# Low parts by a negated copy and an adding transfer instead of a VectorE subtraction, in an attention + bilinear-FFN kernel on one core

## The chip, the core and the metric

The kernel runs on one core of one Trainium2 chip. The metric is the device time of one execution in microseconds (us). Before the change it is 1257.21 us, the median of three runs (1253.98 to 1257.85).

## The reference

```python
# attention: q, k, v are (8, 8, 576, 64); causal by blocks of 64
scores = np.matmul(q, k.transpose(0, 1, 3, 2)) / np.sqrt(D)
scores = np.where(block_i >= block_j, scores, -1e9)
attn = exp(scores - max) / (sum + 1e-09)
x = np.matmul(attn, v)  ->  (4608, 512)
# bilinear feed-forward, d_ff = 1536
a = x @ w_a
b = x @ w_b
out = (a * b) @ w_out            # (4608, 512)
```

Everything is fp32, and the three weights come as doubles of 64 bits that the kernel converts itself.

## The kernel before, in words

**Low parts.** TensorE takes its operands in a rounded form (fp32r). To keep fp32 accuracy, every operand is held twice: a high part, which is the value rounded by ScalarE (a cast), and a low part, which is the value less its high part, by a subtraction on VectorE. A product is then three matmuls: high by high, high by low, low by high. The low parts are made at `split` (L113, of h and of w_out), at L177 and L178 (of the weights and of sums of weights) and at L689 to L692 (of x and sums of x).

**Stages.** For some 640 us attention for 64 heads runs together with the first pass of the feed-forward: tiles of 288 tokens, f 0 to 3 of 12 (f counts blocks of 128 of d_ff). In that pass `ab_unit` makes `h = a*b` (L241 copies a, L243 multiplies to hf, L110 and L113 make hh and hl of it), and `o_unit` multiplies hh and hl by w_out (L217, tile pso). The end of that pass has no attention beside it and runs to about 693 us. Then comes the second stage: two passes of six token tiles of 768 tokens (two halves of 384), pass 0 with f 4 to 7, pass 1 with f 8 to 11. For each f `pair_unit` (L711, tiles psy, psx, psw, psv) makes a and b for both halves with seven products in place of eight, which needs sums of rows of x (seven rows in place of four) and sums of pieces of the weights. VectorE and ScalarE combine the four results to h (L728 to L739). Then `pair_out` (L757, tile pso_z) runs 96 matmuls. In pass 0 the result is added to the DRAM tensor part by transfers that GpSimd issues (L820); in pass 1 SyncE loads part back (L814), VectorE adds it (L822) and SyncE stores the output (L823).

**Sums of x.** `sums_x` works on one of two pairs of the four blocks of 128 rows of x (kp 0 and 1; a block is xr, 128x768). SyncE loads xr (L666) into one of four buffers. VectorE makes four sums of 128x384 (L676, L677, L680, L683; one of them in place), ScalarE casts the seven rows to xh (L681, L682, L684, L685: 768, 768, 768 and 384 columns), and VectorE makes xl by four subtractions of the same sizes (L689 to L692). The next load into a buffer waits for the last reader of what is there.

**Conversion of weights.** A weight tile of 128x512 doubles comes by SyncE (L124, raww). `convert` turns it into fp32 by six instructions, five on VectorE between L139 and L149 and one on ScalarE (L140), through work tiles s, m and x (sw, mw, xw in the profile), with one buffer each. For f 4 and up `sums` reuses m for four sums of 128x128 (L172, four small instructions), ScalarE casts the plain pieces (L165) and the sums (L175) to the high parts, and VectorE subtracts for the low parts (L177 of 128x384, L178 of 128x512). The weights of f 4 to 7, eight such tiles and four of w_out, are converted from the end of attention on: `background` hands out 48 steps as the first pass goes on, one per STEP ns of TensorE time, and what is left beside the first tile of the second stage. Those of f 8 to 11 are converted beside pass 0 in the same way at a slower pace (STEP2), put down in DRAM, and loaded again for pass 1 (`staged`).

**What sets the order.** Each engine runs its own instructions in the order that a scheduler fixes when the kernel is built; it goes by the order in which the code is written and by costs of its own. Nothing overtakes on an engine, so an instruction that waits holds all behind it. An instruction can be held behind others by hand (`behind_of`: conversions and low parts go after the last hf).

Of the kernel before, what the change touches and what calls it, by code (L numbers as in the profile page):

```python
# [11 lines left out]
I32 = mybir.dt.int32  # L12
U16 = mybir.dt.uint16
AF = mybir.ActivationFunctionType
ALU = mybir.AluOpType
AX = mybir.AxisListType

P = 128
# [19 lines left out]
XFB = 2  # L38
MORE = 6
PREF = True  # L40
STEP = 800
STEP2 = 3200
LATE = 1
LO2 = lambda nc: nc.vector
# [8 lines left out]
def attention_then_bilinear_ffn(  # L53
# [10 lines left out]
    nc = tc.nc  # L64
# [34 lines left out]
    wpool = pool(ctx, "wpool", 1)  # L99
# [5 lines left out]
    def f32(ap):  # L105
        return ap.bitcast(F32)

    def split(hi, lo, src, hi_eng, lo_eng):
# [3 lines left out]
            hi_eng.tensor_copy(hi, src)  # L112
        return lo_eng.tensor_tensor(lo, src, f32(hi), op=ALU.subtract)  # L113

    last = {}

    def behind_of(ins, key):
# [9 lines left out]
    def convert(raw, nm, paced):  # L127

        hi, mid = raw[:, :, 1], raw.bitcast(U16)[:, :, 1]
        s, m, x = (wpool.tile([P, 512], I32, tag=f"cv_{x}", name=f"{x}{nm}") for x in "smx")  # L130
        sf, mf, xf = (t.bitcast(F32) for t in (s, m, x))
        v = nc.vector

        def step(ins):
            if paced:
                behind_of(ins, "hf")


        step(v.tensor_scalar(s, hi, 20, 0x7FF, op0=ALU.logical_shift_right, op1=ALU.bitwise_and))  # L139
        nc.scalar.activation(s, s, AF.Relu, scale=2.0 ** 23, bias=shift)  # L140
        yield

        step(v.tensor_scalar(m, hi, 0xFFFFF, 0x100000, op0=ALU.bitwise_and, op1=ALU.bitwise_or))
        yield
        step(v.scalar_tensor_tensor(mf, mid, 2.0 ** -16, m, op0=ALU.mult, op1=ALU.add))
        yield
        step(v.scalar_tensor_tensor(s, hi, -0x80000000, s, op0=ALU.bitwise_and, op1=ALU.bitwise_or))  # L147
        yield
        step(v.tensor_tensor(xf, mf, sf, op=ALU.mult))  # L149
        return xf, mf  # L150
# [7 lines left out]
    def new_wo(f):  # L158
        w_sb[f][1] = wopool.tile([P, 2, DO], F32R, tag="wo", name=f"wo{f}")

    def sums(hi, lo, xf, t, paced):

        x, t = (y.rearrange("p (q n) -> p q n", n=P) for y in (xf, t))
        v = nc.vector
        nc.scalar.copy(hi[:, :3], x[:, 1:])  # L165
        for d, a, b, op in (
            (0, x[:, 0], x[:, 3], ALU.add),
            (1, t[:, 0], x[:, 1], ALU.subtract),
            (2, x[:, 1], x[:, 0], ALU.subtract),
            (3, x[:, 2], t[:, 1], ALU.subtract),  # L170
        ):
            ins = v.tensor_tensor(t[:, d], a, b, op=op)  # L172
        if paced:
            behind_of(ins, "hf")
        nc.scalar.copy(hi[:, 3:], t)  # L175
        yield
        v.tensor_tensor(lo[:, :3], x[:, 1:], f32(hi[:, :3]), op=ALU.subtract)  # L177
        v.tensor_tensor(lo[:, 3:], t, f32(hi[:, 3:]), op=ALU.subtract)  # L178

    def convert_w(todo, lo_eng, paced=False, stage=None):  # L180

        def ahead(f, i):
            return fetch(wab[f, :, i] if i < KP else wo[f], f"w{f}_{i}")

        raw = ahead(*todo[0])
        for k, (f, i) in enumerate(todo):
            now, raw = raw, ahead(*todo[k + 1]) if k + 1 < len(todo) else None
            xf, spare = yield from convert(now, f"w{f}_{i}", paced)
            if stage:
                st = stage.tile([P, 2, NW if i < KP else NO, P], F32R, tag="st", name=f"st{f}_{i}")  # L190
            if i == KP:
                if not stage and w_sb[f][1] is None:
                    new_wo(f)
                o = st.rearrange("p j c n -> p j (c n)") if stage else w_sb[f][1]
                split(o[:, 0], o[:, 1], xf, nc.scalar, lo_eng)
            elif f < F1:
                ab = w_sb[f][0]
                hi, lo = (ab[:, j, i].rearrange("p c n -> p (c n)") for j in range(2))
                split(hi, lo, xf, nc.scalar, lo_eng)
            else:  # L200
                ab = st if stage else w_sb[f][0][:, i]
                yield from sums(ab[:, 0], ab[:, 1], xf, spare, paced)
            if stage:
                f -= F1 + F2
                nc.sync.dma_start(wod[f] if i == KP else wabd[f, i], f32(st).rearrange("p j c n -> p (j c n)"))
            yield
# [463 lines left out]
    def sums_x(raw, kp, nm):  # L670

        hi = xk.tile([P, NW, T2], F32R, tag="xh", name=f"xh_{nm}_{kp}", bufs=3)
        t = tpool.tile([P, 3, T2], F32, tag="xt", name=f"xt_{nm}_{kp}")
        a, b = raw[2 * kp:2 * kp + 2]
        v = nc.vector
# [9 lines left out]
        nc.scalar.copy(hi[:, 6], t[:, 2])  # L685
        yield
        lo = xk.tile([P, NW, T2], F32R, tag="xl", name=f"xl_{nm}_{kp}", bufs=2)
        for ins in (
                v.tensor_tensor(lo[:, 0:2], a, f32(hi[:, 0:2]), op=ALU.subtract),  # L689
                v.tensor_tensor(lo[:, 2:4], t[:, :2], f32(hi[:, 2:4]), op=ALU.subtract),  # L690
                v.tensor_tensor(lo[:, 4:6], b, f32(hi[:, 4:6]), op=ALU.subtract),
                v.tensor_tensor(lo[:, 6], t[:, 2], f32(hi[:, 6]), op=ALU.subtract)):  # L692
            if nm[0] == "0" and nm != "0_0":
                behind_of(ins, "hf")
        yield hi, lo
# [95 lines left out]
    stage = pool(left, "stage", 1, reuse_waits="tile")  # L791
# [113 lines left out]
```

## Time and profile before

| what | value |
|---|---|
| median of the runs | 1257.21 us |
| the profiled execution | 1258.86 us |
| its span | 1257.0 us |
| mean granted clock of TensorE | 0.996 |
| busy PE / PEld / DVE / ACT / POOL | 1231.1 / 1172.9 / 977.1 / 704.2 / 427.7 us |
| from 100 to 600 us (500 us): PE, DVE, ACT, POOL busy | 492.38, 400.83, 401.59, 309.46 us |

PE is TensorE's matmuls and PEld its weight loads; DVE is VectorE, ACT ScalarE, POOL GpSimd, SP SyncE. A row of a timeline has the start, the duration, the engine, the line, the operation and its tiles (out<-in), and in brackets the idle time before it and what ended that. Starts of neighbours in a row lie closer together than their durations, since instructions overlap a little: the distance of two starts is called the pitch. Times count from the start of the span.

### The profile page before, as it was taken

Reading aid. Unit: us, or ns where it says so; the run is one execution under the profiler, and the core shown is the slowest. Engines: PE = TensorE matmul, PEld = TensorE weight load, DVE = VectorE, ACT = ScalarE, POOL = GpSimd, SP = SyncE. Lnnn points to the kernel's source line nnn. Section 1 sums busy time; section 2 is a strip of 40 time slices with the busy share of each in tenths; the row PEclk is TensorE's granted clock in tenths of the full one; section 3 lists DMA queues with packets and bytes.
Section 4 is the critical chain, followed back from the end, with each engine's and each line's share of the span. In section 5 each row is a group of like instructions: output and inputs, shape, how many; then the busy total and the mean of one; then the engine's idle time right before and its main releaser. Section 6 shows DMA issues by size and latency. Waiting matters only on the chain.

```text
span 1257.0 us, 23355 instructions
## 1 busy us (share of the span) xinstructions
PE 1231.1 (98%) x7849; PEld 1172.9 (93%) x7849; DVE 977.1 (78%) x2471; ACT 704.2 (56%) x1770; POOL 427.7 (34%) x597
## 2 busy tenths in 40 slices
PE   9998999999999999999999999999999999999998
PEld 5667999999999999999999999999999999999998
DVE  6888887877878778777789998787868677677654
ACT  4787887787887878878746444244235223222210
POOL 3666665665665656656510021021021000000000
PEclk9899999999999999999999999999999999999999
DMA  5467667776677666776233354464378453143131
GB/s 181 119 182 201 173 174 190 183 178 173 162 186 177 176 172 165 186 177 171 68 121 125 128 147 122 117 164 127 112 210 265 151 151 105 50 148 113 39 101 63
DMA packets 86584, 187.14 MB, mean 149 GB/s; under 512 B 11200, under 2 KB 46016, under 8 KB 86464
## 3 DMA queue, kind: packets, MB, share of 16 engines
q1 hardware_dynamic: 74944, 166.76, 47.5%
q0 software_dynamic: 6912, 9.44, 4.6%
q10 hardware_dynamic: 4608, 9.44, 2.1%
q8 instruction: 63, 1.03, 0.4%
q14 instruction: 57, 0.47, 0.1%
HBM read 87.03 MB, written 47.19 MB: 107 GB/s over the span
## 4 chain that ended last, share of the span: by engine, by line
PE 78%; DVE 11%; DMA 4%; ACT 3%; issue 2%; POOL 2%; SPq 0%; ACTq 0%; DVEq 0%; POOLq 0%
PE pso_z L757 14%; PE ps L217 11%; PE psx_z L711 8%; PE psw_z L711 8%; PE psv_z L711 7%; PE tp L468 7%; PE pso L217 5%; PE s L392 4%; PE psy_z L711 4%; PE av L517 3%; PE av L523 3%; PE sl L392 2%; DMA kp<-kT 2%; DVE nm L398 1%; DVE sw L147 1%
## 5 line engine op out<-in xcount | busy, mean ns | idle before, releaser
L217 PE MATMUL ps<-xh,wab 128*128 128x288 f32 x1024 | 241.7, 304 | 1.2 <-ACT a L241 1.2
L757 PE MATMUL pso_z<-h_z,wo 128*128 128x384 f32 x1152 | 202.3, 335 | 0.0
L757 PEld LDWEIGHTS pso_z<-h_z,wo 128*128 128x128 f32 x1152 | 199.9, 188 | 0.1
L445 POOL TENSOR_SCALAR e<-e,rc 128x512 f32<-128x512 f32 (+3 forms) x256 | 151.1, 602 | 130.2 <-DVE rc L442 122.3
L217 PEld LDWEIGHTS ps<-xh,wab 128*128 128x128 f32 x1024 | 172.1, 189 | 4.7 <-ACT a L241 1.4
L472 DVE TENSOR_TENSOR al<-tp,ah 128x512 fp32r<-128x512 f32 x224 | 131.4, 608 | 30.5 <-ACT ah L470 30.0
L217 PE MATMUL ps<-xl,wab 128*128 128x288 f32 x512 | 154.1, 301 | 0.0
L110 ACT CAST h_z<-u_z 128x384 fp32r<-128x384 f32 x96 | 49.3, 513 | 172.4 <-DVE u_z L736 160.7
L470 ACT CAST ah<-tp 128x512 fp32r<-128x512 f32 x224 | 116.4, 531 | 50.9 <-PE tp L468 47.8
L468 PE MATMUL tp<-ident,e 128*128 128x128 f32 x832 | 134.7, 276 | 9.0 <-POOL e L445 3.0
L820 POOL DMA_DIRECT2D part<-pt x48 | 42.0, 943 | 292.6 <-ACT pt L819 292.2
L217 PE MATMUL pso<-hh,wo 128*128 128x288 f32 x512 | 127.2, 310 | 1.0 <-ACT hh L110 0.8
L468 PEld LDWEIGHTS tp<-ident,e 128*128 128x128 f32 x832 | 99.9, 141 | 23.3 <-issue 10.0
L401 ACT ACTIVATE e<-s,nm 128x192 f32<-128x192 f32 (+2 forms) x192 | 101.4, 528 | 35.9 <-DVE nm L398 26.7
L711 PE MATMUL psx_z<-xh,wab 128*128 128x384 f32 x384 | 116.4, 339 | 2.6 <-DVE u_z L729 2.5
L711 PE MATMUL psv_z<-xh,wab 128*128 128x384 f32 x384 | 116.4, 338 | 1.4 <-DVE u_z L738 0.7
L711 PE MATMUL psw_z<-xh,wab 128*128 128x384 f32 x384 | 116.1, 338 | 0.0
L398 DVE TENSOR_REDUCE nm<-s 128x1 f32<-128x192 f32 (+3 forms) x256 | 109.8, 431 | 2.4
L217 PEld LDWEIGHTS ps<-xl,wab 128*128 128x128 f32 x512 | 96.5, 189 | 3.4
L217 PEld LDWEIGHTS pso<-hh,wo 128*128 128x128 f32 x512 | 88.0, 191 | 2.7 <-ACT hh L110 1.4
L392 PE MATMUL s<-k,q 128*128 128x256 f32 x336 | 81.1, 322 | 2.2 <-ACT e_s L401 2.0
L113 POOL TENSOR_TENSOR v<-vr,v 128x320 fp32r<-128x320 f32 x56 | 50.2, 897 | 88.1 <-ACT v L110 69.4
(143 smaller groups left out, 2872.8 us busy)
## 6 DMA issues: line engine op xcount, KB each, us to landing
k<-kp SPq DMA_DIRECT2D x112, 288.0 KB, 3.6
xr<-xd SPq DMA_DIRECT2D x48, 384.0 KB, 4.0
q<-qp SPq DMA_DIRECT2D x112, 160.0 KB, 2.7
raww<-wab SPq DMA_DIRECT2D x24, 512.0 KB, 3.7
qp<-qT SPq DMA_DIRECT2D x32, 320.0 KB, 3.2
vr<-vm SPq DMA_DIRECT2D x64, 160.0 KB, 3.1
kp<-kT SPq DMA_DIRECT2D x32, 288.0 KB, 3.5
xd<-xf ACTq DMA_DIRECT2D x32, 288.0 KB, 3.1
```

The lines of the kernel that those rows point to most:

```text
L110: nc.scalar.copy(hi, src)
L113: return lo_eng.tensor_tensor(lo, src, f32(hi), op=ALU.subtract)
L217: mm = nc.tensor.matmul(ps, w_, d_, start=(i == 0), stop=(i == n - 1))
L392: mark = nc.tensor.matmul(ps[:, :w], qm[:, q0[t]:q0[t] + P], kk[:, :w], start=(i == 0), stop=(i == len(ks) - 1))
L398: nc.vector.tensor_reduce(nm[:, t:t + 1], view, axis=AX.X, op=ALU.max, negate=True)
L401: nc.scalar.activation(out, view, AF.Exp, bias=bias, accum_out=sm[:, t, :1])
L445: nc.gpsimd.tensor_scalar(ev, ev, rc[:, t:t + 1], 1.0, op0=ALU.mult, op1=ALU.mult)
L468: mark = nc.tensor.transpose(tp[:, c], src, ident)
L470: nc.scalar.copy(ah[:, :m, cols], tp[:, :m])
L472: return nc.vector.tensor_tensor(al[:, :m, cols], tp[:, :m], f32(ah[:, :m, cols]), op=ALU.subtract)
L711: nc.tensor.matmul(ps, wt[:, i, iw], j[:, ix], start=start and kp == 0 and i == 0 and j is xh, stop=kp == KP - 1 and i == 1, skip_group_ch ...
L757: nc.tensor.matmul(ps, wt[:, a, osl], b, start=i == 0, stop=i == 3 * len(fs) - 1)
```

## The change

Where the low part is made by the new helper `low`, ScalarE writes the rounded negative of the value, and a transfer from GpSimd's queue then adds the value itself to that, in place: -round(v) + v is the same low part. This is used at two places: for the second pair of rows of x (kp 1) in all 12 tiles (four subtractions on VectorE each become four ScalarE instructions and four transfers of 384, 384, 384 and 192 KB), and for the sums in the eight weight tiles of f 4 to 7 (L178, 128x512, becomes one ScalarE instruction and one transfer of 256 KB). The low parts of the first pair, of the plain pieces of weights, of w_out, of h and of the staged weights stay subtractions. The work tile m, which the transfers read, gets two buffers in place of one. STEP goes from 800 to 700, so the 48 conversion steps are handed out closer together. The memory for the descriptors of GpSimd's transfers is halved, from 16384 (the default) to 8192 bytes. Lines below the helper move by 5 to 8.

```diff
@@ -38,7 +38,7 @@
 XFB = 2
 MORE = 6
 PREF = True
-STEP = 800
+STEP = 700
 STEP2 = 3200
 LATE = 1
 LO2 = lambda nc: nc.vector
@@ -112,6 +112,11 @@
             hi_eng.tensor_copy(hi, src)
         return lo_eng.tensor_tensor(lo, src, f32(hi), op=ALU.subtract)
 
+    def low(lo, whole):
+
+        nc.scalar.mul(lo, whole, -1.0)
+        nc.gpsimd.dma_start(f32(lo), whole, accum_op=ALU.add)
+
     last = {}
 
     def behind_of(ins, key):
@@ -127,7 +132,7 @@
     def convert(raw, nm, paced):
 
         hi, mid = raw[:, :, 1], raw.bitcast(U16)[:, :, 1]
-        s, m, x = (wpool.tile([P, 512], I32, tag=f"cv_{x}", name=f"{x}{nm}") for x in "smx")
+        s, m, x = (wpool.tile([P, 512], I32, tag=f"cv_{x}", name=f"{x}{nm}", bufs=1 + (x in "m")) for x in "smx")
         sf, mf, xf = (t.bitcast(F32) for t in (s, m, x))
         v = nc.vector
 
@@ -158,7 +163,7 @@
     def new_wo(f):
         w_sb[f][1] = wopool.tile([P, 2, DO], F32R, tag="wo", name=f"wo{f}")
 
-    def sums(hi, lo, xf, t, paced):
+    def sums(hi, lo, xf, t, paced, staged):
 
         x, t = (y.rearrange("p (q n) -> p q n", n=P) for y in (xf, t))
         v = nc.vector
@@ -175,7 +180,10 @@
         nc.scalar.copy(hi[:, 3:], t)
         yield
         v.tensor_tensor(lo[:, :3], x[:, 1:], f32(hi[:, :3]), op=ALU.subtract)
-        v.tensor_tensor(lo[:, 3:], t, f32(hi[:, 3:]), op=ALU.subtract)
+        if staged:
+            v.tensor_tensor(lo[:, 3:], t, f32(hi[:, 3:]), op=ALU.subtract)
+        else:
+            low(lo[:, 3:], t)
 
     def convert_w(todo, lo_eng, paced=False, stage=None):
 
@@ -199,7 +207,7 @@
                 split(hi, lo, xf, nc.scalar, lo_eng)
             else:
                 ab = st if stage else w_sb[f][0][:, i]
-                yield from sums(ab[:, 0], ab[:, 1], xf, spare, paced)
+                yield from sums(ab[:, 0], ab[:, 1], xf, spare, paced, stage)
             if stage:
                 f -= F1 + F2
                 nc.sync.dma_start(wod[f] if i == KP else wabd[f, i], f32(st).rearrange("p j c n -> p (j c n)"))
@@ -685,11 +693,11 @@
         nc.scalar.copy(hi[:, 6], t[:, 2])
         yield
         lo = xk.tile([P, NW, T2], F32R, tag="xl", name=f"xl_{nm}_{kp}", bufs=2)
-        for ins in (
-                v.tensor_tensor(lo[:, 0:2], a, f32(hi[:, 0:2]), op=ALU.subtract),
-                v.tensor_tensor(lo[:, 2:4], t[:, :2], f32(hi[:, 2:4]), op=ALU.subtract),
-                v.tensor_tensor(lo[:, 4:6], b, f32(hi[:, 4:6]), op=ALU.subtract),
-                v.tensor_tensor(lo[:, 6], t[:, 2], f32(hi[:, 6]), op=ALU.subtract)):
+        for at, whole in ((slice(0, 2), a), (slice(2, 4), t[:, :2]), (slice(4, 6), b), (6, t[:, 2])):
+            if kp:
+                low(lo[:, at], whole)
+                continue
+            ins = v.tensor_tensor(lo[:, at], whole, f32(hi[:, at]), op=ALU.subtract)
             if nm[0] == "0" and nm != "0_0":
                 behind_of(ins, "hf")
         yield hi, lo
@@ -892,7 +900,7 @@
                     .reshape(NF, P, NCC // 2, -1)).view(np.int64),
         "wo": flat(moe_w_out.reshape(NF, P, -1)).view(np.int64),
     }
-    nc = bacc.Bacc("TRN2", target_bir_lowering=False, num_devices=1)
+    nc = bacc.Bacc("TRN2", target_bir_lowering=False, num_devices=1, dynamic_dma_scratch_size=8192)
     args = [
         nc.dram_tensor(n, a.shape, mybir.dt.from_np(a.dtype), kind="ExternalInput").ap()
         for n, a in arrays.items()
```

VectorE's row has 56 instructions fewer, ScalarE's and GpSimd's 56 more each, SyncE's as many as before.

On VectorE in the second conversion (tile 1 of f 4, at about 651 to 656 us in the trace; `mw_1`, `sw_1`, `xw_1` are its work tiles, `mw_0` and `sw_0` those of the conversions next to it), before:

```order
L147 SCALAR_TENSOR_TENSOR sw_1_9941<-raww_1_9860,sw_1_9941 128x512
L680 TENSOR_TENSOR xt_0_0_10466<-xr_0_9851,xr_0_9849 128x384
L149 TENSOR_TENSOR xw_1_9943<-mw_1_9942,sw_1_9941 128x512
L683 TENSOR_TENSOR xt_0_0_10466<-xr_0_9851,xt_0_0_10466 128x384
L172 TENSOR_TENSOR mw_1_9942<-xw_1_9943 128x128 x2
L172 TENSOR_TENSOR mw_1_9942<-mw_1_9942,xw_1_9943 128x128
L177 TENSOR_TENSOR wab_9845<-xw_1_9943,wab_9845 128x384
L172 TENSOR_TENSOR mw_1_9942<-xw_1_9943,mw_1_9942 128x128
L139 TENSOR_SCALAR sw_0_10015<-raww_0_9939 128x512
L676 TENSOR_TENSOR xt_0_1_10481<-xr_0_9855,xr_0_9853 128x384
L178 TENSOR_TENSOR wab_9845<-mw_1_9942,wab_9845 128x512
```

and now, with what each instruction waits for (`DMASW0` is the landing of the first transfer into wab, issued for `mw_0_9863`):

```order
L152 SCALAR_TENSOR_TENSOR sw_1_9934<-raww_1_9860,sw_1_9934 128x512
L113 TENSOR_TENSOR hl_0_0_9962<-hf_0_0_9959,hh_0_0_9961 128x288 [waits Activation_49]
L154 TENSOR_TENSOR xw_1_9936<-mw_1_9935,sw_1_9934 128x512 [waits DVE_49]
L148 TENSOR_SCALAR mw_0_10004<-raww_0_9932 128x512 [waits DMAHW6_49,DMASW0_49]
L177 TENSOR_TENSOR mw_1_9935<-xw_1_9936 128x128 [waits DVE_49]
L177 TENSOR_TENSOR mw_1_9935<-xw_1_9936 128x128
L177 TENSOR_TENSOR mw_1_9935<-mw_1_9935,xw_1_9936 128x128 [waits DVE_49]
L182 TENSOR_TENSOR wab_9845<-xw_1_9936,wab_9845 128x384 [waits Activation_49]
L177 TENSOR_TENSOR mw_1_9935<-xw_1_9936,mw_1_9935 128x128 [waits DVE_49]
L144 TENSOR_SCALAR sw_0_10003<-raww_0_9932 128x512
```

The subtraction L178 is gone, and the first write of the third conversion's m stands ahead of the second conversion's sums; it waits for the transfer that reads the first conversion's m.

On VectorE at the end of the first pass (hl_1_3 is the last low part of h there; `xl_0_0` and `xl_0_1` are the low parts of the first tile of x), before:

```order
L243 TENSOR_TENSOR hf_1_3_10448<-ps_7_1_3_10426,a_1_3_10424 128x288
L143 TENSOR_SCALAR mw_1_10388<-raww_1_10309 128x512
L147 SCALAR_TENSOR_TENSOR sw_1_10387<-raww_1_10309,sw_1_10387 128x512
L145 SCALAR_TENSOR_TENSOR mw_1_10388<-raww_1_10309,mw_1_10388 128x512
L113 TENSOR_TENSOR hl_1_3_10451<-hf_1_3_10448,hh_1_3_10450 128x288
L149 TENSOR_TENSOR xw_1_10389<-mw_1_10388,sw_1_10387 128x512
L689 TENSOR_TENSOR xl_0_0_10475<-xr_0_9849,xh_0_0_10465 128x768
L172 TENSOR_TENSOR mw_1_10388<-xw_1_10389 128x128 x2
L172 TENSOR_TENSOR mw_1_10388<-mw_1_10388,xw_1_10389 128x128
L177 TENSOR_TENSOR wab_9848<-xw_1_10389,wab_9848 128x384
L172 TENSOR_TENSOR mw_1_10388<-xw_1_10389,mw_1_10388 128x128
```

and now:

```order
L177 TENSOR_TENSOR mw_1_10347<-xw_1_10348,mw_1_10347 128x128
L113 TENSOR_TENSOR hl_1_2_10425<-hf_1_2_10422,hh_1_2_10424 128x288
L251 TENSOR_TENSOR hf_1_3_10456<-ps_7_1_3_10443,a_1_3_10441 128x288
L144 TENSOR_SCALAR sw_2_10578<-raww_2_10344 128x512
L148 TENSOR_SCALAR mw_2_10579<-raww_2_10344 128x512
L150 SCALAR_TENSOR_TENSOR mw_2_10579<-raww_2_10344,mw_2_10579 128x512
L113 TENSOR_TENSOR hl_1_3_10459<-hf_1_3_10456,hh_1_3_10458 128x288
L700 TENSOR_TENSOR xl_0_0_10483<-xr_0_9849,xh_0_0_10473 128x768
L700 TENSOR_TENSOR xl_0_0_10483<-xt_0_0_10474,xh_0_0_10473 128x768
L700 TENSOR_TENSOR xl_0_0_10483<-xr_0_9851,xh_0_0_10473 128x768
L700 TENSOR_TENSOR xl_0_0_10483<-xt_0_0_10474,xh_0_0_10473 128x384
```

The last of the eight conversions (into wab_9848) now stands ahead of the last hf and hl, behind which it stood before, and the first of w_out has begun. The four subtractions for xl_0_1, which followed those for xl_0_0, are gone.

On SyncE in a tile of pass 1 (`xr_3` are the four blocks of x for the tile after the next: 14350, 14352 the first pair and 14354, 14356 the second), before:

```order
L666 DMA xr_3_14350<-xd 128x768
L666 DMA xr_3_14352<-xd 128x768
L666 DMA xr_3_14354<-xd 128x768
L666 DMA xr_3_14356<-xd 128x768
L823 DMA outT<-pt_0_1_1_13989 128x384
L823 DMA outT<-pt_1_1_1_13991 128x384
L823 DMA outT<-pt_2_1_1_13993 128x384
L823 DMA outT<-pt_3_1_1_13995 128x384
```

and now:

```order
L674 DMA xr_3_14394<-xd 128x768
L674 DMA xr_3_14396<-xd 128x768
L831 DMA outT<-pt_0_1_1_14029 128x384
L831 DMA outT<-pt_1_1_1_14031 128x384
L674 DMA xr_3_14398<-xd 128x768
L822 DMA pt_2_1_1_14230<-part 128x384
L822 DMA pt_3_1_1_14237<-part 128x384
L831 DMA outT<-pt_2_1_1_14033 128x384
L831 DMA outT<-pt_3_1_1_14035 128x384
L674 DMA xr_3_14400<-xd 128x768
```

The two loads of the second pair, whose buffers are now read by the adding transfers, stand behind stores of the output and loads of part.

## Prediction

> **What bounds the kernel now.** The page's first part comes first, then the busy time by stretches, PE's waits in the second stage, and the timelines of PE and DVE where those waits lie.
>
> ```profile
> PE 1231.1 (98%) x7849; PEld 1172.9 (93%) x7849; DVE 977.1 (78%) x2471; ACT 704.2 (56%) x1770; POOL 427.7 (34%) x597
> ...
> 640.00:660.00 20.00, 19.49 (x145) 19.04 (x144) 19.53 (x44) 8.51 (x21) 2.17 (x2) 1.00 0.33 105
> 660.00:680.00 20.00, 20.00 (x151) 19.79 (x150) 19.51 (x49) 10.83 (x25) 0.00 (x0) 1.00 0.39 128
> 680.00:700.00 20.00, 18.40 (x113) 17.93 (x112) 19.32 (x41) 12.60 (x25) 0.00 (x0) 0.91 0.49 162
> 700.00:720.00 20.00, 18.48 (x104) 17.39 (x103) 19.79 (x41) 6.80 (x12) 0.00 (x0) 1.00 0.32 106
> ...
> 1000.00:1050.00 50.00, 50.00 (x287) 50.00 (x286) 34.77 (x64) 11.72 (x21) 0.00 (x0) 1.00 0.33 95
> ```
>
> The columns of a stretch are its length, then busy time of PE, PEld, DVE, ACT, POOL, then PE's clock. PE is the bound nearly everywhere. Only from 680 to 720 us does it idle, 1.6 + 1.5 us, and there its clock is at 0.91 for one slice, which costs 20 x 0.09 = 1.8 us more. From 640 to 720 us DVE is full (19.3 to 19.8 of 20): that is where the weights of f 4 to 7 are converted beside the end of the first pass. Late in the second stage DVE has 15 us of 50 free, and work taken from it there is worth nothing by itself.
>
> ```profile
> PE psx_z L711 <- DVE u_z L729: 2.5, 2, 1.6
> PE pso L217 <- DVE hl L113: 1.1, 2, 0.8
> PE pso L217 <- ACT hh L110: 0.8, 1, 0.8
> PE psv_z L711 <- DVE u_z L738: 0.7, 1, 0.7
> PE psv_z L711 <- ACT u_z L728: 0.7, 1, 0.7
> ...
> 684.67 0.40 PE L217 MATMUL pso<-hl,wo 128*128 128x288 f32 x1 [0.77 <-DVE hl L113]
> ...
> 686.29 0.66 PE L217 MATMUL pso<-hh,wo 128*128 128x288 f32 x3 [0.83 <-ACT hh L110]
> ```
>
> The waits after 640 us come to 5.8 us (total, times, longest). With the slow slice that is some 7.6 us, and no relief of DVE can give more than this. The two waits of the timeline, at 684 to 686, are for h's parts, which stand behind conversions on DVE.
>
> **The change, part by part.** The durations are those of the profiled execution, which took 1258.86 us (span 1257.0); it lies 1.65 above the median of 1257.21.
>
> *Weights (8 conversions, f 4 to 7).* First the pitch of the steps on DVE:
>
> ```profile
> 646.71 0.28 DVE L172 TENSOR_TENSOR mw<-xw,mw 128x128 f32<-128x128 f32 x1
> ...
> 660.27 0.55 DVE L177 TENSOR_TENSOR wab<-xw,wab 128x384 fp32r<-128x384 f32 x1
> 660.74 0.28 DVE L172 TENSOR_TENSOR mw<-xw,mw 128x128 f32<-128x128 f32 x1
> 660.94 0.42 DVE L139 TENSOR_SCALAR sw<-raww 128x512 int32<-128x512 int32 x1
> 661.28 0.45 DVE L113 TENSOR_TENSOR hl<-hf,hh 128x288 fp32r<-128x288 f32 x1
> 661.65 0.55 DVE L683 TENSOR_TENSOR xt<-xr,xt 128x384 f32<-128x384 f32 x1
> 662.12 0.68 DVE L178 TENSOR_TENSOR wab<-mw,wab 128x512 fp32r<-128x512 f32 x1
> 662.72 0.68 DVE L147 SCALAR_TENSOR_TENSOR sw<-raww,sw 128x512 int32<-128x512 int32 x1
> ...
> 687.11 0.45 DVE L113 TENSOR_TENSOR hl<-hf,hh 128x288 fp32r<-128x288 f32 x1
> 688.08 0.95 DVE L689 TENSOR_TENSOR xl<-xr,xh 128x768 fp32r<-128x768 f32 x1
> ...
> L175 ACT CAST wab<-mw 128x512 fp32r<-128x512 f32 x8 | 5.0, 620 | 4.4 <-DVE mw L172 4.4
> ```
>
> From start to start L178 occupies 0.60 us, so 8 x 0.60 = 4.8 us leave DVE. In its place ACT does a second pass over 128x512, 0.62 like the cast of L175 (pipelined 0.52), and POOL sends 256 KB. But the transfer still reads m. The next writer of that buffer, two conversions on, waits for it to land, and everything behind that writer on DVE waits too, h's parts of the first pass among it. I walked the changed order of DVE with the pitches above (0.34 for the 128x512 tensor-scalar, 0.60 for 128x512, 0.47 for 128x384, 0.37 for 128x288, 0.20 for 128x128). From the last sum of one conversion to the write of the same buffer lie 4.9, 4.0, 5.3, 5.7, 4.8, 4.1, 5.9, 5.5 us of work. The loop to be covered is 0.1 + 0.52 + 0.52 on ACT plus issue to landing.
>
> No accumulate into the on-chip memory is in the trace. The nearest rows are those into part:
>
> ```profile
> part<-pt POOLq DMA_DIRECT2D x1, 192.0 KB, 4.4
> ...
> part<-pt POOLq DMA_DIRECT2D x1, 192.0 KB, 5.0
> ...
> part<-pt POOLq DMA_DIRECT2D x1, 192.0 KB, 5.2
> ...
> part<-pt POOLq DMA_DIRECT2D x1, 192.0 KB, 7.8
> ...
> 731.64 3.71 POOL L820 DMA_DIRECT2D part<-pt  x4 [87.32 <-ACT pt L819]
> 735.84 0.86 POOL L820 DMA_DIRECT2D part<-pt  x1 [0.49 <-ACT pt L819]
> ```
>
> The DMA issues, looked at one by one, give from issue to landing 4.4 for the one at 731.64, 5.0 and 5.2 for those that come after an idle queue at 776.54 and 916.93, and 7.8 for the fifth of the burst, at 735.84. So a lone one takes 4.4 to 5.2. A burst drains at (735.84 + 7.8 - 731.64 - 4.4) / 4 = 1.9 us each. I take 5.0: more bytes, but a nearer target than DRAM. The loop is then 6.1 us, and the stalls are 1.2, 2.1, 0.8, 0, 1.3, 0.7, 0, 0.6 (a stall that both ends share counts once). 6.1 of these 6.7 us come ahead of the last h. At 4.4 it is 3.7 us, at 2.9 or less nothing, at 6.4 about 11.
>
> The work between the end of the first conversion and the end of the last hl is 38.0 us in the new order against 40.6 before (646.91 to 687.48): one subtraction per conversion is gone, but STEP 700 puts more conversion steps ahead of it. So the last hh and hl come 6.1 - 2.6 = 3.5 us later, and hh another 0.7 for a cast of x that now stands ahead of it on ACT. **PE's first pass ends 4.2 us later.** Bounds: -2.6 (no stall) and +9. While it lasts PE runs with gaps and may lose clock as it does at 680 to 700; that is taken as in before.
>
> By the Trainium skill ("DMA: Bandwidth & Descriptors", Anatomy of one DMA) a transfer from GpSimd takes 2.0 us plus its bytes over 436 KB per us, an estimate of 2.6 us for 256 KB and 2.45 for 192 KB. The rows above show twice the latter, so the trace disagrees, but for DRAM and an accumulate only; by the page's figure there would be no stall, and the sum would be that of the first rival.
>
> *First tile of x (B).* Its second half of low parts leaves DVE, 3 x 0.87 + 0.47 = 3.1 us:
>
> ```profile
> 695.64 0.55 DVE L692 TENSOR_TENSOR xl<-xt,xh 128x384 fp32r<-128x384 f32 x1
> ...
> 686.15 0.83 ACT L682 CAST xh<-xt 128x768 fp32r<-128x768 f32 x1
> 686.88 0.83 ACT L684 CAST xh<-xr 128x768 fp32r<-128x768 f32 x1
> ...
> L711 PEld LDWEIGHTS psy_z<-xl,wab x96: 187/188/190, 692.8 to 1229.7; 128*128 128x128 f32 x96
> ```
>
> Before, it was complete at 696.1. Now the sum of the last conversion ends 35.6 us of work and 6.1 of stalls behind 646.91, at 688.6, and its cast and copy on ACT at 689.7. Then come eight casts of x and one of h (0.73 each by the two rows, 0.42 for the short ones), to 695.3, and four negated copies, the first done at 696.0. The first transfer lands at 701.0, the others 1.9 to 2.6 apart (the larger for twice the bytes), the short one at up to 708. PE began this stage at 692.8, now at 697.0; it has 21 matmuls of 0.174 (50.00 us by 287) that need no low part of the second pair, and wants the first at 701 and the last at 703. It waits some 3 to 4 us: **+3.5**. Bounds 0 and +7.
>
> *Later tiles (C).* Eleven times 3.1 us leave DVE, and as much goes to ACT, which has room (11.7 of 50 busy). Worth at most the 0.9 and 1.6 of PE's wait for L729. Against it: the raw rows of the second pair are now read by the transfers, and the next load into them waits for their landing.
>
> ```profile
> 1146.27 0.51 ACT L685 CAST xh<-xt 128x384 fp32r<-128x384 f32 x1
> ...
> 1156.12 0.56 DVE L676 TENSOR_TENSOR xt<-xr,xr 128x384 f32<-128x384 f32 x1 [0.53 <-DMA xr<-xd]
> ...
> 1163.53 0.56 DVE L729 TENSOR_TENSOR u_z<-psx_z,u_z 128x384 f32<-128x384 f32 x1 [2.07 <-ACT u_z L728]
> ...
> 1164.85 0.34 PE L711 MATMUL psx_z<-xh,wab 128*128 128x384 f32 x1
> ...
> 1144.61 7.48 SPq L666 DMA_DIRECT2D xr<-xd  x4
> ...
> DMA to landing us min/median/max: 3.1/4.0/7.2
> ```
>
> ACT's casts of that pair end at 1146.8, so the first copy is done at 1147.5 and its transfer lands at 1152.5; the third, the last reader of the late raw buffer, lands 3.8 to 5.2 behind it, at 1156.3 to 1157.7. SP's load follows and takes about 4: 1160.3 to 1161.7, where before L676 had its rows at 1156.1. Behind it on DVE stand four sums and two adds of pt, 6 x 0.47 = 2.8 us, ahead of what was L729: it starts at 1163.1 to 1164.5, against 1163.5 before and 1164.3 at which PE needs it to start (the matmul at 1164.85 writes where it reads). So 0 to 0.2 a tile in pass 1, four tiles; in pass 0, five tiles, where loads take as long as 7.2 and POOL's queue also holds the sends to part, 0 to 3, of which I take 0.6. That is +3.5, less the 2.5 lost before: **+1**. Bounds -2.5 and +20.
>
> *The rest.* The smaller ring for descriptors and the order in attention: nothing, within 1 us. PE has the same order there, and at most five transfers are in flight.
>
> Sum: 4.2 + 3.5 + 1 = 8.7, and 1258.86 + 8.7 - 1.65 = 1265.9; I give **1265.5**.
>
> **Rivals.** What a measurement can tell from no change is about 0.3%, or 3.8 us: 1253.4 to 1261.0.
>
> 1. *The transfers land within about 3 us* since they stay on the chip. Then no stall; the last h comes 2.6 us sooner, PE loses neither the 1.6 of idling nor most of the slow slice (-3.3), B is 0, and of the 2.5 in later tiles most is saved: -5, which is 1252. Every accumulate in the trace speaks against it, but none has this target. The point from which it decides is a landing of 2.9 us. This is the case of the Trainium skill's figure above. Chance 0.27.
> 2. *No measurable change*, 1257: landing near 4 us, stalls of 2 to 3 us in the conversions equal to what is saved, B hidden. The row with 4.4 speaks for it. Chance 0.21.
> 3. *The transfers' rate sets the tiles.* If a burst of 384 KB drains at 3 to 4 us each, up to twice the row's 1.9, the third lands at 1158.5 to 1160.5 and what was L729 starts at 1165.3 to 1167.3, 1.0 to 3.0 too late in each of nine tiles: +9 to +27, with A and a B of 6 to 8 in all +20 to +40, or 1277 to 1297. For: the bytes of a transfer double. Against: the bytes need not be what takes those 1.9 us. Chance 0.14.
>
> The forecast itself, 1261 to 1275, has 0.38. **Range** 1251.5 to 1286: it takes in most of rivals 1 and 2 and the lower half of 3. Within the likeliest case alone it is 1261 to 1275. **Chances:** faster 0.27, within 0.3% 0.21, slower 0.52.
>
> **What would show it.** Right: in the changed profile DVE idles some 1 to 2 us ahead of writes of mw between 650 and 695, released by the transfer into wab; PE's wait for hh and hl grows at 685 to 692; PE waits for xl in the first tile; from issue to landing the new transfers show about 5 us. Wrong: landings near 3 us and DVE without those gaps (rival 1); PE waits for u_z in every tile, and xr's loads land after L729's turn (rival 3); gaps in PE ahead of 640 us would speak of something I have costed at nothing.

## The result and the profile after

The changed kernel takes 1331.64 us (median of four runs, 1327.71 to 1331.91) against 1257.08 before (median of four, one run more than stood ahead): a ratio of 1.0593, with a 95% interval of 1.0574 to 1.0613. That is 74.6 us slower, far above the forecast of 1265.5 and its upper end of 1286. The profiled execution has a span of 1330.1 us. The busy line of the page after, and the stretch from 640 us to the end, of before and of after (length, then busy time of PE, PEld, DVE, ACT, POOL, then PE's clock, the DMA engines' share and GB/s):

```profile
PE 1252.6 (94%) x7849; PEld 1190.9 (90%) x7849; DVE 937.3 (70%) x2415; ACT 737.4 (55%) x1826; POOL 478.8 (36%) x653
```

```profile
640.00:1257.00 617.00, 607.28 (x3531) 603.86 (x3529) 471.87 (x917) 206.53 (x385) 44.13 (x50) 1.00 0.44 128
```

```profile
640.00:1331.00 691.00, 630.30 (x3534) 623.12 (x3532) 435.47 (x863) 239.39 (x441) 94.42 (x106) 0.96 0.53 141
```

DVE did get its relief (471.9 to 435.5 us). But PE, with the same matmuls, now idles 691.0 - 630.3 = 60.7 us where it idled 9.7, and is busy 23.0 us longer, at a mean clock of 0.96. The waits of PE from 640 us on (total, times, longest):

```profile
PE psx_z L719 <- DVE u_z L737: 43.9, 9, 6.4
PE psy_z L719 <- DMA xl<-xt: 3.8, 2, 2.6
PE psv_z L719 <- DVE u_z L746: 3.3, 1, 3.3
PE pso L225 <- ACT hh L110: 2.7, 3, 0.9
PE psw_z L719 <- DVE u_z L743: 1.2, 1, 1.2
PE pso L225 <- DVE hl L113: 0.7, 1, 0.7
```

Nine waits for the first addition of a tile (L737, L729 before) hold 43.9 of 55.6 us: four in pass 0, one at the start of pass 1, four in pass 1. The starts of the first matmul of pso_z in each tile divide the time into stages, in us:

| stage | before | after | weights only | raw on VectorE | six buffers and held sums |
|---|---|---|---|---|---|
| start of the second stage | 692.8 | 696.2 | 695.8 | 694.8 | 693.7 |
| first tile, to its pso_z | 28.4 | 35.6 | 27.8 | 33.1 | 35.6 |
| five tiles of pass 0 | 234.2 | 263.2 | 235.5 | 234.5 | 242.5 |
| from pass 0 to pass 1 | 49.5 | 59.3 | 49.5 | 53.1 | 52.1 |
| five tiles of pass 1 | 231.6 | 255.3 | 231.6 | 231.6 | 231.6 |
| from the last pso_z to the end | 20.4 | 20.4 | 20.4 | 20.4 | 20.4 |

(The last three columns are experiments, told below.) The tiles of x carry 69.7 of the 73.1 us by which the spans differ, the conversions 3.4.

One tile of pass 1 shows how; its pso_z starts at 1106.3. First POOL's and SP's rows, then single issues of the DMA view (out<-in, KB, us from issue to landing: the transfer issued at 1112.07 and the load at 1123.01), then DVE and PE, and last the stretch behind PE's wait (columns as above).

```profile
1110.18 0.86 POOL L118 DMA_DIRECT2D xl<-xr  x1 [48.34 <-DMA xr<-xd]
1110.92 1.02 POOL L118 DMA_DIRECT2D xl<-xt  x1
1112.07 0.88 POOL L118 DMA_DIRECT2D xl<-xr  x1
1112.61 1.24 POOL L118 DMA_DIRECT2D xl<-xt  x1
...
1106.96 3.89 SPq L674 DMA_DIRECT2D xr<-xd  x2
1112.11 1.73 SPq L831 DMA_DIRECT2D outT<-pt  x2
1116.22 0.33 SPq L674 DMA_DIRECT2D xr<-xd  x1
1119.80 2.15 SPq L822 DMA_DIRECT2D pt<-part  x2
1122.04 0.87 SPq L831 DMA_DIRECT2D outT<-pt  x2
1123.01 1.14 SPq L674 DMA_DIRECT2D xr<-xd  x1
...
xl<-xr POOLq DMA_DIRECT2D x1, 384.0 KB, 9.0
...
xr<-xd SPq DMA_DIRECT2D x1, 384.0 KB, 4.6
...
1127.78 0.56 DVE L684 TENSOR_TENSOR xt<-xr,xr 128x384 f32<-128x384 f32 x1 [8.21 <-DMA xr<-xd]
1130.84 0.54 DVE L737 TENSOR_TENSOR u_z<-psx_z,u_z 128x384 f32<-128x384 f32 x1
...
1127.04 0.34 PE L719 MATMUL psv_z<-xh,wab 128*128 128x384 f32 x1
1131.44 0.69 PE L719 MATMUL psx_z<-xh,wab 128*128 128x384 f32 x1 [4.06 <-DVE u_z L737]
...
1136.72 0.52 PE L719 MATMUL psv_z<-xl,wab 128*128 128x384 f32 x1
1137.04 0.52 PE L719 MATMUL psv_z<-xh,wab 128*128 128x384 f32 x1
...
1138.47 0.34 PE L719 MATMUL psx_z<-xh,wab 128*128 128x384 f32 x1
...
1131.40:1137.40 6.00, 5.96 (x19) 5.96 (x20) 2.23 (x4) 0.51 (x1) 0.00 (x0) 0.50 0.46 136
```

The third transfer, the last reader of the late raw buffer, is issued at 1112.07 and lands 9.0 later, at 1121.0. SP could load into that buffer then, but stands at loads of part and stores of the output until 1123.01. (Those loads of part wait for the stores of 1112.11 and 1112.57, which went among the transfers and land 7.7 and 9.0 us after their issue; the stores at the same place of the kernel before, at 1152.64 to 1154.08, land in 3.9.) The load lands 4.6 later. All this time DVE idles, 8.21 us, at the first sum that needs it, with the addition that PE waits for behind it in the row. Four sums and two adds take another 3.1 us, and PE has waited 4.06 us. Then its matmuls come 0.32 us apart for about 6 us (durations 0.52 in place of 0.34) before they are at 0.176 again: the granted clock was 0.50 in that stretch.

### The profile page after: what moved, and what is told of

Same layout as the page of the kernel before. It is cut to its first block, busy times and chain, and to the rows that moved or that the text cites. A ratio compares the mean times of both kernels' runs of the same rounds, so it can differ in the third digit from the quotient of the medians.

```text
span 1330.1 us, 23517 instructions
## 1 busy us (share of the span) xinstructions
PE 1252.6 (94%) x7849; PEld 1190.9 (90%) x7849; DVE 937.3 (70%) x2415; ACT 737.4 (55%) x1826; POOL 478.8 (36%) x653
## 4 chain that ended last, share of the span: by engine, by line
PE 59%; DMA 14%; issue 10%; DVE 9%; ACT 5%; POOL 2%; SPq 1%; DVEq 0%; ACTq 0%; POOLq 0%
PE ps L225 11%; PE pso_z L765 7%; PE tp L476 6%; PE psx_z L719 5%; PE psw_z L719 5%; PE psv_z L719 5%; PE pso L225 4%; DMA outT<-pt 4%; DMA xr<-xd 4%; PE s L400 3%; PE av L531 2%; PE av L525 2%; PE psy_z L719 2%; DMA xl<-xr 2%; PE sl L400 2%
## 5 line engine op out<-in xcount | busy, mean ns | idle before, releaser
L118 POOL DMA_DIRECT2D xl<-xr x24 | 23.0, 958 | 454.3 <-DVE xl L700 182.5
L719 PE MATMUL psx_z<-xh,wab 128*128 128x384 f32 x384 | 123.7, 359 | 43.9 <-DVE u_z L737 43.9
L719 PE MATMUL psw_z<-xh,wab 128*128 128x384 f32 x384 | 121.7, 353 | 1.2 <-DVE u_z L743 1.2
L476 PEld LDWEIGHTS tp<-ident,e 128*128 128x128 f32 x832 | 99.7, 140 | 23.8 <-issue 10.4
L719 PEld LDWEIGHTS psx_z<-xh,wab 128*128 128x128 f32 x384 | 75.8, 200 | 47.2 <-DVE u_z L737 47.1
L406 DVE TENSOR_REDUCE nm<-s 128x1 f32<-128x128 f32 (+3 forms) x256 | 109.8, 430 | 2.3
```

The source lines that it names most:

```text
L406: nc.vector.tensor_reduce(nm[:, t:t + 1], view, axis=AX.X, op=ALU.max, negate=True)
L476: mark = nc.tensor.transpose(tp[:, c], src, ident)
L719: nc.tensor.matmul(ps, wt[:, i, iw], j[:, ix], start=start and kp == 0 and i == 0 and j is xh, stop=kp == KP - 1 and i == 1, skip_group_ch ...
```

## The experiments

Three theories stood against each other. **Theory 1**, the chain: raw rows come free only when transfers land, SP's load and DVE's row wait for that, PE behind them. **Theory 2**, the traffic: the transfers slow all others, wherever they are waited for. **Theory 3**: it is the weights' part, STEP or the descriptor memory.

### One part alone

*Weights only.* In `sums_x`, `if kp:` became `if False:`.

> The second pair of x goes back to subtractions on VectorE; the transfers for the weights, STEP 700, two buffers of m and the smaller descriptor memory stay. Theory 1 (reload chain: the loads of raw x wait for the adding transfers, and VectorE's row waits with them) expects 1252 to 1262 us, with no wait of PE for the first u_z of a tile over 2 us. Theory 2 (the transfers' traffic slows the other transfers in general) expects the same within some us, since only 2 of 18.6 MB of them are left. Theory 3 (the weights, STEP or the descriptor memory carry the loss) expects over 1300.

Measured: 1259.06 against 1256.71, ratio 1.0023 (1.0007 to 1.0039). The tiles are back at the times of before, within 1.3 us (table); the waits of PE for L737 are 2.1 us in all.

*x only.*

The cuts of the edit ("..." stands for what is left out, within a line too):

```diff
-STEP = 700
+STEP = 800
...
-        s, m, x = (wpool.tile(..., bufs=1 + (x in "m")) for x in "smx")
+        s, m, x = (wpool.tile(..., bufs=1) for x in "smx")
...
-        if staged:
+        if True:
             v.tensor_tensor(lo[:, 3:], t, f32(hi[:, 3:]), op=ALU.subtract)
...
-    nc = bacc.Bacc(..., dynamic_dma_scratch_size=8192)
+    nc = bacc.Bacc(...)
```

> Only the second pair of x by transfers; weights on VectorE, STEP 800, one buffer of m, descriptor memory as before the change. Theory 1 expects 1322 to 1338, nine waits of 4 to 6 us for the first u_z of a tile. Theory 2 expects the same. Theory 3 expects below 1275.

Measured: 1327.17, ratio 1.056 (1.0536 to 1.0583); nine waits for L737 of 46.9 us in all (3.8 to 7.1 each, where 4 to 6 was expected). Theory 3 falls: the transfers for x carry the loss alone, and the descriptor memory had no share in it, since it was the old one here.

### Cutting the chain in different places

*Raw rows on VectorE.* Only the two transfers of each tile that read sums are left; the ones that read raw rows are subtractions again.

```diff
-            if kp:
+            if kp and whole is not a and whole is not b:
```

> As the changed kernel, but the low parts of the two raw blocks of the second pair are subtracted on VectorE again; only the sums' low parts (768 and 384 columns a tile) go by transfers. The raw buffers then come free by VectorE. Theory 1 expects 1254 to 1268 and no PE wait for u_z over 2 us in the tiles. Theory 2 (traffic) expects about half of the loss, some 1290 to 1300, since some 40 per cent of the bytes are left.

Measured: 1269.59, ratio 1.01 (1.0073 to 1.0127). PE's waits from 640 us on:

```profile
PE psx_z L719 <- DVE u_z L737: 4.2, 3, 2.1
PE psy_z L719 <- DMA xl<-xt: 3.0, 1, 3.0
```

With 1152 of a tile's 2688 columns still sent by transfers (43 per cent), the five tiles of pass 1 take what they took before, and those of pass 0 nearly. The 12.9 us left lie in the first tile (where PE waits 3.0 us for the transfer itself, that is, for xl), at the start of pass 1 and in the conversions. At the start of pass 1 it is the same kind of chain at another buffer: DVE's first sum waits 5.08 us until the transfer that reads the earlier sums in its buffer has landed, and PE 2.1 us behind it. It came out 1.6 us above theory 1's range, and 20 below theory 2's.

*Held sums.* All transfers stay; the chain stays as long; only what stands behind it on DVE changes:

```diff
             if nm == f"0_{NT2}":
                 behind_of(ins, "hf")
+            elif kp:
+                behind_of(ins, "u1")
...
-        v.tensor_tensor(u, x, u, op=ALU.add)
+        u1 = v.tensor_tensor(u, x, u, op=ALU.add)
+        if halves:
+            last["u1"] = u1
```

(`halves` is true for the first f of a tile, and u1 is its first addition, L737; the two instructions held are the first two sums of the second pair.)

> As the changed kernel with all transfers, but on VectorE the first two sums of the second pair of the tile after next are held behind the first additions of the first f of the next tile, so that a late load of raw x holds nothing that PE waits for. Theory 1 expects the waits for u_z to fall from 44 us to under 10 and 1262 to 1285. Theory 2 expects no more than 10 us of gain (1320 or more), since loads and transfers are as slow as before.

Measured: 1285.1, ratio 1.0241 (1.0208 to 1.0274). The waits of PE:

```profile
PE psw_z L721 <- DVE u_z L743: 8.5, 7, 2.5
PE psx_z L721 <- DVE u_z L739: 6.6, 4, 3.9
```

(L737 is L739 here, and L743 the second addition.) The first sum had gone behind the first addition but ahead of the next ones in the order, so seven tiles still wait, 0.3 to 2.5 us for the second one; the tiles of pass 0 also wait 0.5 to 3.9 us for the first. The waits for u_z come to 15.1 us in these two lines, where theory 1 expected under 10, and the time is at the upper edge of its range. Theory 2's 1320 is 35 us off. (The profiled execution took 1294.52 us, the longest of the four.)

*Six raw buffers.* `2 * KP` became `2 * KP + 2` in rpool.

> As the changed kernel, with six buffers for raw rows of x in place of four, so that a load has a free buffer earlier: the second pair's loads no longer wait for the transfers of the tile just before, but half of the loads (the first pair of the tile after) move on to do so. Theory 1 (reload chain) expects PE's waits for the first u_z to fall from 44 us to under 15 and 1262 to 1285. Theory 2 (the traffic of the transfers slows everything) expects 1315 or more.

Measured: 1283.7, ratio 1.0218 (1.0187 to 1.0248); the waits for L737 are 13.9 us (nine, the longest 6.3, at the end of pass 0). That is what theory 1 expected: a load with a free buffer comes in time, with every transfer still there.

*Both together.*

> Six raw buffers and the sums of the second pair held behind the first additions of the next tile, together: all transfers stay. If the two remedies work on the same chain (1285 each), and what is left is waits elsewhere (first tile, last f of pass 0, the refill of raw rows): 1268 to 1282. If the rest is the transfers' traffic on the queues and on the engines: no lower than 1280.

Measured: 1277.92, ratio 1.0158 (1.0139 to 1.0176). The time alone is 2 us below what theory 2 allows; the tiles of pass 1 say more. Three of them, of the changed kernel and of this one:

```profile
1106.30:1263.30 157.00, 144.61 (x795) 143.64 (x794) 89.84 (x169) 42.15 (x73) 10.51 (x12) 0.96 0.45 117
```

```profile
1070.20:1209.10 138.90, 138.90 (x793) 138.90 (x792) 88.89 (x169) 41.63 (x73) 10.53 (x12) 1.00 0.50 127
```

The same instructions on every engine, twelve transfers on POOL in both; in the second PE is busy without a gap, at 46.3 us a tile as in the kernel before. So in these tiles the transfers' traffic costs PE nothing once nothing that PE needs stands behind a late load. What a tile lost, (157.0 - 138.9) / 3 = 6.0 us, is 12.4 / 3 = 4.1 of idling and 1.9 of slow clock (144.61 - 138.90 over three). What is left of this kernel's 20.7 us is in the first tile, at the end of pass 0 and at the start of pass 1.

At the end of pass 0 (a tile of 54.7 us, 47.8 before, with a wait of 6.3) it is not the raw rows. ACT and DVE in this kernel:

```profile
898.95 0.51 ACT L170 CAST st<-xw 128x384 fp32r<-128x384 f32 x1 [6.95 <-DMA wabd<-st]
...
899.50 0.56 DVE L182 TENSOR_TENSOR st<-xw,st 128x384 fp32r<-128x384 f32 x1 [12.36 <-ACT st L170]
```

The conversion of a staged weight waits for the store of the one before, which went at 888.08 among the transfers and lands 10.8 us later (4.4 at the same place of the kernel before, at 880.39), and the first addition stands behind it on DVE. (In the changed kernel the same kind of store holds DVE until 919.19 in that tile, and the raw rows come 1.5 us later.) There theory 2 is right: a transfer that has nothing to do with x is slow, and it is waited for. Nor are the two theories exclusive in the other tiles, since the traffic makes the links of the chain longer: the stores of the output named above, and the first transfer of the tile shown, 6.0 us beside a load of x against 4.0 in the last tile, which has none. The runs show that the chain, through DVE's order, turns late landings into waits of PE. How much of the lateness is the chain's links and how much the traffic, no run separates.

### Other ways around it

*First pair instead of the second.* `if kp:` became `if not kp:`.

> The transfers make the low parts of the first pair of x in place of the second; all else as in the changed kernel: the same number, sizes and kinds of instructions. The first pair's transfers can go some 2 to 4 us earlier in a tile and its loads stand first on SyncE, but PE wants this pair first. Theory 1 expects the waits for u_z to shrink to under 2 us a tile, with perhaps new waits for xl: 1262 to 1295. Theory 2 expects no change against the changed kernel, within 8 us.

Measured: 1287.86, ratio 1.0259 (1.0227 to 1.0291). The same instructions cost 31 us in place of 75. In the five tiles of pass 1 they cost 0.5 us (232.1 against 231.6). Three things differ there: these transfers go earlier in the tile; SP's four loads again stand together; and no load runs beside the first of them. In a tile of pass 1, those issued from 1076.57 on land 4.0, 5.5, 6.7 and 8.0 us after their issue, where those of the tile shown took 6.0, 7.6, 9.0 and 10.4. No run tells the three apart. In pass 0 the waits stay at 1.6 to 4.0 us, with 7.2 at the start of pass 1, where theory 1 expected under 2. Theory 2's "no change" is off by 44 us.

*Loads on GpSimd.* To take SP's 2.0 us out of the chain, the second pair's loads went to the queue that has just sent the transfers:

```diff
-            nc.sync.dma_start(
+            (nc.gpsimd if cc >= 2 and xs else nc.sync).dma_start(
                 raw[cc]...
```

> As the changed kernel, but the loads of the second pair's raw rows from the second tile on are issued by GpSimd in place of SyncE, behind the transfers that they wait for anyway, so that they no longer stand behind stores of the output and loads of part. If SyncE's row holds the load by some 2.5 us (as in one tile of the trace), PE's waits for u_z in pass 1 fall from 4.1 to about 2 a tile and the time to 1305 to 1322. If the transfers' landing alone sets the load, no change in pass 1. In pass 0 the loads can now hold GpSimd's sends to part, which may cost as much again.

Measured: 1346.17, ratio 1.0711 (1.0682 to 1.0739). The gain, 1305 to 1322, did not come. In pass 0 the waits grew from some 5.8 us to 8.3 and up to 11.6, as feared, and at the start of pass 1 from 4.4 to 9.5. In pass 1 they stayed, at 3.4 to 4.1 us, as expected if the landing alone sets the load, but for another reason:

```profile
1132.10 0.57 POOL L674 DMA_DIRECT2D xr<-xd  x1 [2.31 <-DMA xl<-xr]
1136.97 0.56 POOL L674 DMA_DIRECT2D xr<-xd  x1 [4.30 <-DMA xl<-xr]
...
1142.95 0.56 DVE L684 TENSOR_TENSOR xt<-xr,xr 128x384 f32<-128x384 f32 x1 [9.74 <-DMA xr<-xd]
```

The load now goes 0.3 us after the transfer, issued at 1128.01, has landed (8.7 later), but itself takes 5.9 us in place of 4.6.

### The weights' part, and what to keep

*STEP 700 alone* (the kernel before with STEP 700):

> Only STEP 700 in place of 800; no transfers, one buffer of m, the old descriptor memory. It tells whether part of the 2.3 us by which the last low part of h came later in the conversions is STEP's. If the waits for the transfers make all of it: within 2 us of the kernel before. If the denser conversions make it: 2 to 4 us slower.

Measured: 1257.12 against 1257.26, ratio 1.001 (0.9991 to 1.003).

*Weights only, three buffers of m, STEP 800:*

> Only the weights by transfers, with three buffers of m and STEP 800; so no write of m waits for a transfer. If those waits (2.7 us in the trace) and STEP carry the 2.9 us that the weights part costs: 1252 to 1257, as fast as before or a little faster. If it is the longer chain behind the sums: the same 1259.

Measured: 1255.75, ratio 0.9989 (0.997 to 1.0009): no difference that can be told from the kernel before, where the form with two buffers and STEP 700 had 1.0023. The two intervals overlap, and which of the two edits makes the difference, if there is one, is not separated.

*The least harmful form with transfers for x* (raw rows on VectorE, held sums, three buffers of m, STEP 800):

> The least harmful form found so far with transfers for x left in: only the sums' low parts of the second pair go by transfers, the sums of the second pair are held behind the first additions of the next tile, m has three buffers and STEP is 800. If transfers for x can be had without loss: 1252 to 1259. If their chain always costs something: 1260 to 1270, as without these remedies.

Measured: 1259.57, ratio 1.0016 (1.0002 to 1.003). This lies between the two ranges, 0.6 us above the first. Nearly all of the loss can be had back, and nothing is gained: PE waits 3.3 us for xl in the first tile, and at most 1.3 for anything after that.

*Weights by transfers, three buffers of m, STEP 800, held sums, no transfer for x:*

> What the other runs leave as harmless, and the one edit that could help the kernel before as well: only the weights by transfers, three buffers of m, STEP 800, no transfer for x, and the sums of the second pair held behind the first additions of the next tile. The wait for u_z at the second tile or at the fifth of pass 0 (0.9 and 1.6 us before) should go: 1252 to 1256. If it only exchanges waits, 1256 to 1259, as fast as before.

Measured: 1253.81 against 1257.71, ratio 0.9962 (0.9948 to 0.9977). This beats the kernel before by 0.4 per cent. PE's waits from 640 us on:

```profile
PE pso L225 <- ACT hh L110: 1.6, 2, 1.5
PE psv_z L721 <- DVE u_z L745: 1.1, 1, 1.1
PE pso L225 <- DVE hl L113: 0.8, 2, 0.6
PE psx_z L721 <- DVE u_z L739: 0.4, 1, 0.4
```

They come to 3.9 us against 5.8 before. In the place that was named, 0.4 us of the 2.5 for the first addition are left (2.0 in the run without held sums), and the five tiles of pass 0 take 232.2 us against 234.2 (233.8). The intervals of the runs with and without held sums, 0.9948 to 0.9977 and 0.997 to 1.0009, still touch, and the kernel before was not run with held sums alone, so the gain is not shown to be theirs.

## Why the prediction was wrong

**What bounds the kernel** was right: PE, with at most 7.6 us to be won. The relief of DVE was worth nothing beyond that (36 us less work from 640 us on, 73 us more time).

**Conversions (A), +4.2: near in the sum, by two errors that offset each other.** The second stage begins 3.4 us later. Since the attention ahead of it varies by as much, the better measure is the stretch from the first conversion's last sum to the last hl: 42.7 us (647.22 to 689.93) against 40.4 (646.71 to 687.11), 2.3 later where 3.5 was forecast. The landing, DVE's waits in that stretch, and its busy time:

```profile
wab<-mw POOLq DMA_DIRECT2D x1, 256.0 KB, 3.5
...
DVE mw L148 <- DMA wab<-mw: 2.7, 3, 1.4
DVE sw L152 <- ACT sw L145: 0.6, 2, 0.4
...
647.40:690.30 42.90, 39.01 (x278) 36.98 (x277) 39.16 (x100) 26.26 (x57) 7.02 (x8) 1.00 0.63 164
...
646.90:687.50 40.60, 38.49 (x281) 37.36 (x280) 40.05 (x99) 21.77 (x48) 0.00 (x0) 0.99 0.35 114
```

(The last row is of before. DVE's busy time is 39.16 against 40.05.) The eight accumulates within the chip land 3.2 to 4.3 us after their issue, not 5.0. The writes of m wait 2.7 us for them, not 6.1. But the row held 0.9 us less work than before, not 2.6 less. That the two misses nearly cancel was luck. By the Trainium skill ("DMA: Bandwidth & Descriptors", Anatomy of one DMA) an estimate for the transfer is 2.6 us. The trace does not bear that out either, though it lies nearer than my 5.0 from DRAM.

**First tile (B), +3.5: measured +7.2.** The transfers were not the wait that I named: PE waits 1.2 us for xl. The rest comes by SP's row, which I had not followed there:

```profile
700.16 1.27 SPq L674 DMA_DIRECT2D xr<-xd  x1
701.52 1.24 SPq L129 DMA_DIRECT2D raww<-wo  x1
705.12 0.32 SPq L674 DMA_DIRECT2D xr<-xd  x1
706.11 0.33 SPq L129 DMA_DIRECT2D raww<-wo  x1
...
709.76 0.43 DVE L148 TENSOR_SCALAR mw<-raww 128x512 int32<-128x512 int32 x1 [2.61 <-DMA raww<-wo]
...
712.25 0.55 DVE L743 TENSOR_TENSOR u_z<-psw_z,u_z 128x384 f32<-128x384 f32 x1
```

A load of w_out stands behind a load of x that waits for a transfer, and itself takes 8.2 us (701.52 to 709.74); DVE waits 2.61 us for it with additions behind it, and PE 1.2 and 3.3 us for those. In the run with weights only this tile takes 27.8 us, so the transfers for x make it.

**Later tiles (C), "0 to 0.2 a tile in pass 1 ... of which I take 0.6 ... +1": this step failed, by over 60 us.** The stages of the later tiles grew by 29.0, 9.8 and 23.7, 62.5 us in all. The chain was seen, and rival 3 had its mechanism, but its links were each priced at their least. Set against the tile above (its times are 37.7 lower than those of before that the prediction used):

| link | predicted | measured |
|---|---|---|
| third transfer lands | 1118.6 to 1120.0 | 1121.0 |
| SP issues the load | the same moment | 1123.0 |
| the load has landed | 1122.6 to 1124.0 | 1127.6 |
| the addition L737 starts | 1125.4 to 1126.8 | 1130.84 |
| PE needs it to start | 1126.6 | 1126.6 |

The transfers came 2.5 us apart, within the range taken; but the first of them took 6.0 us in place of 5.0, with a load of x, issued at 1110.54, beside it. The two steps that were left out altogether are SP's row (2.0 us), although the order quoted with the change showed the load behind stores and loads of part, and the clock. The waits of 3.6 to 4.7 us in the tiles of pass 1 cost another 1.5 to 2.7 each (53.1 - 46.3 - 4.06 = 2.7 in the tile shown), and that was reckoned nowhere but in the first pass.

In pass 0 the waits are 5.2 to 6.4 us, beyond the 0 to 3 that was allowed. There SP's row is not the reason, as the first of these tiles shows (the load's landing comes from the DMA view):

```profile
748.20 0.32 SPq L674 DMA_DIRECT2D xr<-xd  x1
...
xr<-xd SPq DMA_DIRECT2D x1, 384.0 KB, 9.9
...
758.24 0.56 DVE L684 TENSOR_TENSOR xt<-xr,xr 128x384 f32<-128x384 f32 x1 [9.44 <-DMA xr<-xd]
...
761.10 0.69 PE L719 MATMUL psx_z<-xh,wab 128*128 128x384 f32 x1 [6.12 <-DVE u_z L737]
```

The third transfer landed at 748.15, and the load went at once; it was the load itself that took 9.9 us. The last loads of the four tiles with a wait take 7.6 to 10.4 us, among sends to part and weights, where the same loads took 5.8 to 6.8 before and the prediction went by 7.2 at most.

**Rival 3** named the chain but not its price: 1.0 to 3.0 a tile, 1277 to 1297 in all, against 6.0 in pass 1 and 29.0 over the five tiles of pass 0, four of which have such a wait. Its cause, transfers at 3 to 4 us apart, was not the cause: in the tile shown they land 2.4, 2.5 and 1.9 us apart. That I gave it 0.14 follows from the same omission. Rivals 1 and 2 rested on an early landing; that came, nearly (3.2 to 4.3 us), and it only decided the part that hardly mattered.

**The rest at nothing** holds for STEP (1.001) and for the descriptor memory (its old size did not help). The attention stage differs by several us between kernels whose order there is nearly the same: the second stage starts at 689.6 in the run with x only and at 700.0 in the run with held sums.

## What to carry to other kernels

A transfer that reads a buffer keeps it until it lands, so moving an operation from a compute engine to a DMA also moves the release of its inputs: follow that release through the next load, the row of the queue that issues it, and whatever the consumer engine has queued behind the first instruction that needs the load. Price the whole chain against the slack of the engine that bounds the kernel, with loads and stores as slow as they get among the new transfers, add the slow clock to each of its waits of more than some two us, and ask whether the engine that is relieved was in anybody's way. Where it is too long, an instruction held back so that nothing urgent stands behind it gives back most (46 of 75 us here), without touching the chain.

## What the runs showed of the hardware

Accumulating transfers within the chip land 3.2 to 4.3 us after their issue when one goes at a time (256 KB), and 4.0 us with 384 KB and no load beside. In the burst shown they land 2.4 and 2.5 us apart with 384 KB and 1.9 apart for the last, which has half the bytes; that one has landed 10.4 us after its issue. Stores and loads that go among such a burst land late: 7.7 and 9.0 us where it was 3.9, and 10.8 where it was 4.4.

The PE wait of 4.06 us was followed by matmuls 0.32 us apart in place of 0.176, at a granted clock of 0.50; the stretch at 0.50 is 6.8 us long there and 3.4 us behind the other three waits of the tiles of pass 1. By the Trainium skill ("TensorE: Matmul & The Clock Gate", Part 1) an idle window of about 3.4 us halves the clock, and as long a busy one restores it. The traces agree with the half clock and with the length, once or twice 3.4 us. A shorter wait can do it, though: in the run with weights only, 2.05 us at 750 was followed by 3.4 us at 0.50, while in the run with six raw buffers 2.77 us at 999 was not. Waits of 0.3 to 1.4 us in pass 1 of the run with held sums left the clock at 1.00.
